# Strassen's algorithm in the last two token tiles of an attention and feed-forward kernel

## The chip, the core and the metric

The kernel runs on one core of one Trainium2 chip. The metric is the device time in microseconds of one launch; the time of the kernel before is the median of seven runs. The profile is that of one execution. Engines are written as in the profile: PE (TensorE, matrix multiplication; PEld is its weight load), DVE (VectorE), ACT (ScalarE), POOL (GpSimd), SP (SyncE, which issues the DMAs here).

## What is computed

```python
batch, n_heads, seq, head_dim = (8, 8, 576, 64)
# attention: heads 0-3 with a local mask of 32 positions, heads 4-7 with a strided one
scores = np.where(masks[None], scale * np.matmul(q, k.transpose(0, 1, 3, 2)), -1000000000.0)
attn = softmax(scores)
x = np.matmul(attn, v).transpose(0, 2, 1, 3).reshape(B * S, H * D)      # 4608 x 512
# feed-forward
a = x @ w1            # 512 x 1024
b = x @ w2            # 512 x 1024
h = a * b @ w3        # 1024 x 1024
out = h @ w_out       # 1024 x 512, float32
```

Inputs and output are float32. The kernel computes with fp16 operands and float32 sums, and multiplies w3 by w_out first, since nothing stands between them; the feed-forward part is then (a * b) @ w34.

## The kernel before

**Layout.** The attention output is kept transposed as `xT`, four tiles of 128 channels (one pair of heads each) by 4608 tokens. The weights are `w1h` and `w2h` (four chunks of 128 channels by 1024) and `w34` (eight blocks of 128 d_ff rows by 512). The feed-forward part goes over nine tiles of 512 tokens (loop at line 940). A tile has eight d_ff blocks `jc`. For each block, `ps_a` is summed over four matmuls of 128x512 (line 956), copied to SBUF by ACT (`asb`, line 964, traced at its helper's line 309), `ps_b` is summed over four more (line 972), and DVE multiplies the two into `abt` (line 978). Then four output pieces of eight matmuls each (line 992) are copied to `osb` by ACT and stored by SP (line 1013). A batch has 576 tokens, so tile 7 (tokens 3584 to 4095) reads batches 6 and 7 and tile 8 (4096 to 4607) reads batch 7 alone.

**Attention.** For each of eight batches (line 689) and four pairs of heads: scores on PE (line 794), exp on ACT (lines 808 and 811), mask on DVE (line 818), the product with v on PE (lines 830 and 840), and the normalisation. For the strided pairs that is a logarithm and an exp on ACT (lines 874 and 885) and two DVE multiplications into `xT` (line 901); for the local ones DVE (lines 863 and 864), a transpose on PE (line 921) and a copy. q, k and v arrive as float32 in staging tiles `stgs` (eight of 128x1024 float32), and POOL casts nearly all of them to fp16 (traced at line 313).

**Order.** Nothing in the order is left to chance: `Plan` (line 54) holds every piece of work as an `Op` with an estimated duration for each engine that may take it, its dependencies, the buffers that it takes and gives back, and a rank. `Plan.order` (line 89) walks through time with these estimates; whenever an engine is free it takes, among the operations that are ready and have their buffers, the one of lowest rank (lines 176 to 188). The sequence that comes out is emitted and each engine keeps to it. Matmuls marked `soft` have to have been ready for 100 ns by the estimates (`slack`, line 182). Operations marked `lock` on DVE and POOL are laid one after the other (line 212).

**Ranks.** Tile t has rank 100 + 24 t + 2 jc + 1 for the a matmuls of block jc (line 959), just above it for b, and 100 + 24 t + 17 + 2 ts for output piece ts (line 998). Attention of batch b has ranks from `_arank` (line 19), which lay the four head pairs over the span of the tile that is computed meanwhile.

**PSUM.** Eight banks: four single ones (kind "f", used by a, b and output matmuls among others) and two pairs (kind "B", scores and attention products). An "f" bank of `ps_a` comes free with the copy, one of `ps_b` with the multiplication.

## Time and profile before

| what | value |
|---|---|
| median of seven runs | 273.12 us |
| lowest and highest | 271.87 and 275.29 us |
| the profiled execution | 271.87 us |
| its span | 270.2 us |
| granted clock of PE over the span | 1.0 |
| PE, busy and share of the span | 258.9 us, 96% |
| DVE | 169.7 us, 63% |
| ACT | 156.0 us, 58% |
| POOL | 146.3 us, 54% |
| chain that ended last: share on PE | 83% |
| a, b and output matmuls' shares in that chain | 22%, 22%, 21% |

How to read it: the span is what the profiler saw of the program, and the time of the same execution is 1.7 us longer. An engine's busy time is the sum of its instructions; where it is under 100%, the rest is waiting or having nothing to do. A row of the profile names a line, an engine, an operation, what it writes and reads, shapes, and a count; then the busy time in us, the mean duration of one in ns, and the engine's idle time just ahead of them with what ended it. Matmuls overlap: a row's mean (379 ns for a 128x512 one) is longer than the distance between two starts, and the distance is what PE can do. Times in the instruction lists are start and length in us.

### The profile page before, as it was taken

Reading aid. Unit: us, or ns where it says so; the run is one execution under the profiler, and the core shown is the slowest. Engines: PE = TensorE matmul, PEld = TensorE weight load, DVE = VectorE, ACT = ScalarE, POOL = GpSimd, SP = SyncE. Lnnn points to the kernel's source line nnn. Section 1 sums busy time; section 2 is a strip of 40 time slices with the busy share of each in tenths; the row PEclk is TensorE's granted clock in tenths of the full one; section 3 lists DMA queues with packets and bytes.
Section 4 is the critical chain, followed back from the end, with each engine's and each line's share of the span. In section 5 each row is a group of like instructions: output and inputs, shape, how many; then the busy total and the mean of one; then the engine's idle time right before and its main releaser. Section 6 shows DMA issues by size and latency. Waiting matters only on the chain.

```text
span 270.2 us, 6083 instructions
## 1 busy us (share of the span) xinstructions
PE 258.9 (96%) x2265; PEld 141.3 (52%) x2265; DVE 169.7 (63%) x324; ACT 156.0 (58%) x280; POOL 146.3 (54%) x172
## 2 busy tenths in 40 slices
PE   7787899999999999999999999999999999999994
PEld 2466787545565555544544554455455554444443
DVE  6745566885787758766884788487669762422321
ACT  2770467764676764775577647756764774333331
POOL 6676996689979447955794289626980000000000
PEclk9999999999999999999999999999999999999999
DMA  7999999999799899899999998999996013003004
GB/s 244 336 359 284 307 361 353 317 252 292 266 271 227 135 273 217 197 182 290 194 196 197 273 169 198 173 276 199 194 208 139 0 41 116 2 21 136 0 4 155
DMA packets 72766, 54.41 MB, mean 201 GB/s; under 512 B 44256, under 2 KB 62048, under 8 KB 72736
## 3 DMA queue, kind: packets, MB, share of 16 engines
q1 hardware_dynamic: 72736, 54.02, 82.1%
q8 instruction: 18, 0.29, 0.5%
q14 instruction: 12, 0.10, 0.2%
HBM read 38.93 MB, written 9.44 MB: 179 GB/s over the span
## 4 chain that ended last, share of the span: by engine, by line
PE 83%; DMA 9%; issue 2%; ACT 2%; POOL 1%; SPq 1%; DVE 1%; POOLq 0%; ACTq 0%
PE ps_b L972 22%; PE ps_a L956 22%; PE ps_o L992 21%; DMA st<-in_moe_w_dram 5%; PE ps_S L794 4%; PE ps_mm L669 3%; PE ps_X L840 3%; PE ps_X L830 2%; PE ps_U L921 2%; DMA st<-in_k_dram 2%; DMA out_dram<-osb 2%; PE ps_T L747 1%; SPq L316 1%; POOL w3n L313 1%; PE ps_tr L649 1%
## 5 line engine op out<-in xcount | busy, mean ns | idle before, releaser
L972 PE MATMUL ps_b<-xT,w2h 128*128 128x512 f16 x288 | 73.8, 379 | 0.2 <-DVE kTL L311 0.2
L956 PE MATMUL ps_a<-xT,w1h 128*128 128x512 f16 x288 | 73.9, 379 | 0.0
L978 DVE TENSOR_TENSOR abt<-ps_b,asb 128x512 f16<-128x512 f32 x72 | 49.7, 690 | 38.4 <-PE ps_b L972 35.5
L309 ACT COPY asb<-ps_a 128x512 f32<-128x512 f32 x72 | 42.1, 586 | 49.5 <-PE ps_a L956 49.2
L992 PE MATMUL ps_o<-w,abt 128*128 128x512 f16 (+2 forms) x304 | 67.3, 368 | 0.0
L313 POOL CAST xs<-st 80x1024 f16<-80x1024 f32 (+1 forms) x36 | 33.4, 941 | 19.5 <-DMA st<-in_q_dram 16.7
L972 PEld LDWEIGHTS <-w2h 128*128 128x128 f16 x288 | 26.7, 98 | 28.6 <-issue 0.7
L992 PEld LDWEIGHTS <-abt 128*128 128x128 f16 x304 | 27.2, 98 | 27.6
L956 PEld LDWEIGHTS <-w1h 128*128 128x128 f16 x288 | 26.5, 98 | 27.5
L811 ACT ACTIVATE ps_S<-ps_S 128x576 f32<-128x576 f32 (+2 forms) x56 | 32.9, 627 | 12.2 <-PE ps_S L794 11.6
L309 ACT COPY osb<-ps_o 128x512 f32<-128x512 f32 (+1 forms) x36 | 20.8, 577 | 23.8 <-PE ps_o L992 21.0
L901 DVE TENSOR_TENSOR xT<-ps_X,rcp 64x288 f16<-64x288 f32 x56 | 25.2, 450 | 13.6 <-ACT rcp L885 12.8
L313 POOL CAST v16L<-st 32x768 f16<-32x768 f32 (+1 forms) x32 | 26.3, 821 | 6.6 <-DMA st<-in_v_dram 3.8
L818 DVE TENSOR_TENSOR ptm<-ps_S,maskL 128x576 f16<-128x576 f32 x28 | 19.9, 751 | 9.4 <-ACT ps_S L811 9.3
L864 DVE TENSOR_TENSOR xqs<-ps_X,rcq 96x384 f16<-96x384 f32 (+1 forms) x36 | 20.5, 568 | 1.2
L313 POOL CAST v16S<-st 72x1024 f16<-72x1024 f32 (+1 forms) x16 | 16.4, 1035 | 6.0 <-DMA st<-in_v_dram 6.0
L885 ACT ACTIVATE rcp<-ps_X 64x576 f32<-64x576 f32 x28 | 18.1, 647 | 0.9
L874 ACT ACTIVATE ps_X<-ps_X 64x576 f32<-64x576 f32 x28 | 17.7, 632 | 0.3
L669 PE MATMUL ps_mm<-woh,xT 128*128 128x256 f16 x128 | 16.0, 273 | 1.5 <-POOL woh L313 1.5
L840 PEld LDWEIGHTS <-ptm 128*96 128x96 f16 (+1 forms) x224 | 14.5, 124 | 5.5 <-issue 0.2
L313 POOL CAST x<-st 128x1024 f16<-128x1024 f32 x14 | 14.4, 1037 | 3.8 <-DMA st<-in_q_dram 1.9
L311 DVE COPY xT<-ps_U 128x576 f16<-128x576 f16 x18 | 8.8, 490 | 11.3 <-PE ps_U L921 11.3
(82 smaller groups left out, 265.9 us busy)
## 6 DMA issues: line engine op xcount, KB each, us to landing
out_dram<-osb SPq DMA_DIRECT2D x35, 256.0 KB
st<-in_moe_w_dram SPq DMA_DIRECT2D x16, 512.0 KB
st<-in_v_dram SPq DMA_DIRECT2D x16, 288.0 KB
st<-in_v_dram SPq DMA_DIRECT2D x16, 256.0 KB
st<-in_q_dram SPq DMA_DIRECT2D x7, 512.0 KB
st<-in_k_dram SPq DMA_DIRECT2D x7, 512.0 KB
st<-in_q_dram SPq DMA_DIRECT2D x10, 256.0 KB
st<-in_k_dram SPq DMA_DIRECT2D x10, 256.0 KB
```

The source lines that it names most:

```text
L309: pin(nc.scalar.copy(out=out, in_=in_))
L313: pin(nc.gpsimd.tensor_copy(out=out, in_=in_))
L669: pin(nc.tensor.matmul(ps, w3T(kc)[:, js], big["woh"][:, kc, ns], start=(kc == 0), stop=(kc == KF - 1)))
L811: pin(nc.scalar.activation(out=sps, in_=sps, func=AF.Exp, bias=0.0, scale=scale))
L818: pin(nc.vector.tensor_mul(ptm[0:kr, 0:576].rearrange("p (h a x) -> p h a x", h=2, x=w), pte[0:kr].rearrange("p h (a x) -> p h a x", x=w), ...
L840: pin(nc.tensor.matmul(xps[0:w, h, i * 65:(i + 1) * 65], ptms[pslot][0:kr, c0:c0 + w], vt[0:kr, 2 * (hp % 2) + h, g * m + i, 0:D + 1], sta ...
L864: pin(nc.vector.tensor_mul(xqs[0:w, 0:m].rearrange("p i h d -> p h i d"), xv[:, :, :, 0:D], _ap(rcp, 0, [[rcp.ap[0][0], w], [4, 2], [1, m] ...
L901: pin(nc.vector.tensor_mul(o, i0, i1))
L956: pin(nc.tensor.matmul(ps, w1h[:, ci, js], xT[ci][:, tok], start=(ci == 0), stop=(ci == KM - 1)))
L972: pin(nc.tensor.matmul(ps, w2h[:, ci, js], xT[ci][:, tok], start=(ci == 0), stop=(ci == KM - 1)))
L978: pin(nc.vector.tensor_mul(big[("abt", t)][:, jc, :], bank("f", f"b{t}_{jc}"), live[("asb", t, jc)]))
L992: pin(nc.tensor.matmul(ps, big[("abt", t)][:, ci, bass.ds(ts * P, P)], w34[:, ci, bass.ds(n0, nw)], start=(ci == 0), stop=(ci == KF - 1)))
```

## The change

Tiles 7 and 8 (`tA` and `tB`) are computed together. With X11, X12 the two channel halves of tile 7, X21, X22 those of tile 8, and W the matrix with w1 and w2 side by side, split in its channel halves, the four blocks a(7), b(7), a(8), b(8) are a 2x2 product of 2x2 blocks. For seven of the eight d_ff blocks (1 to 7; `sf`) it is formed in the way of Strassen and Winograd, with seven products of two matmuls in place of eight. Block 0 of both tiles stays as it was.

- **Sums of weights** T1 to T4 (fp16, 128x2x1024, kept in staging tiles), each in two halves of 512 columns, all on POOL. The first halves (columns for blocks 1 to 3) depend on the last load, the second halves (blocks 4 to 7) on a `gate`, a small POOL copy that depends on the last sum of inputs.
- **Sums of inputs** S1 to S4 (fp16, 128x2x512 each, in two pieces c): both pieces of S3 and the first pieces of S1, S2 and S4 on POOL, the second pieces of S1, S2 and S4 on DVE. They need `xT` of batch 7 and 6.
- **Products** P1 to P7: P1, P6, P7 and P4 are added up in one "f" bank (A); P5 and then P3 in one half of a "B" pair (G); P2 in the other (E). Between them: ACT copies A after P1 (`e`; in blocks 1 and 2 to SBUF, later straight into E), after P6 (`u2`), G after P5 (`p5`) and, from block 3 on, E after P2 (`c11`). DVE adds `u2` to G in place (`u4`), `p5` to A into SBUF (`c22`), in blocks 1 and 2 also the copy to E (`c11`), and multiplies: `h1` = G times c11 into tile 7's `abt`, `h2` = A times c22 into tile 8's. P6 waits for e, P7 for u2, P3 for u4, P4 for c22. The "B" pair is held from P5 to h1, the "f" bank from P1 to h2.
- **Ranks.** Block n (0 to 6) of the Strassen stage starts at 268 + 3n; block 0 of tile 7 has 269, that of tile 8 has 293; the output matmuls of both tiles are put 16 further back and also depend on every P5. The attention of batches 2 to 7 is moved back by 2.
- The new branch `xb` for the attention products' bank keeps to "B" with this configuration.

```diff
-    base = {0: 40, 1: 60}.get(b, 100 + 24 * (b - 1) - 4)
+    base = {0: 40, 1: 60}.get(b, 100 + 24 * (b - 1) - 2)
...
-           first=('DVE', 'ACT', 'POOL'), early=0, pm=4, nx=4, nstg=8, new=(2, 3), lb=3, ll=4, nat={'POOL': 1160})
+           first=('DVE', 'ACT', 'POOL'), early=0, pm=4, nx=4, nstg=8, new=(2, 3), lb=3, ll=4, nat={'POOL': 1160}, sf=(1, 2, 3, 4, 5, 6, 7), te={'POOL': 2150}, nr=(1, 25, 2, 0), te1='POOL', se=((3, 0), (3, 1), (1, 0), (2, 0), (4, 0)))
...
-    plan = Plan(dict(f=NF, B=2, stg=NSTG, asb=2, osb=3, rcp=2, xqs=2, xqd=cfg.get("nxq", 2), w3n=3, abt=NABT))
+    plan = Plan(dict(f=NF, B=2, stg=NSTG, asb=2, osb=3, rcp=2, xqs=2, xqd=cfg.get("nxq", 2), w3n=3, abt=NABT,
+                     u2=2, p5=2, c11=2, c22=2))
...
+    SF = cfg.get("sf", ())
+    tA, tB = NTILE - 2, NTILE - 1
+    tk1, tk2 = bass.ds(tA * NT, NT), bass.ds(tB * NT, NT)
+    smul, sfirst = {}, []
+    if SF:
+        W = {(1, 1): w1h[:, 0:2], (1, 2): w2h[:, 0:2], (2, 1): w1h[:, 2:4], (2, 2): w2h[:, 2:4]}
+        T, Tt = {}, {}
+        scr = consts.tile([P, 2], FP16, name="scr")
+        lastload = plan.loads[-1]
+        allw = [c for jc in range(KF) for c in w1c[jc] + w2c[jc]]
+        hw = DF // 2
+        for i, x, y in ((1, (1, 2), (1, 1)), (3, (2, 2), (1, 2)), (2, (2, 2), 1), (4, (2, 1), 2)):
+            for hf in range(2):
+                cs = bass.ds(hf * hw, hw)
+                def ftt(e, i=i, x=x, y=y, cs=cs, hf=hf):
+                    if hf == 0:
+                        Tt[i] = stgs[plan.slot[("stg", f"T{i}")]].bitcast(FP16).rearrange("p (k n) -> p k n", k=2)
+                    b0 = Tt[y] if isinstance(y, int) else W[y]
+                    eng = nc.gpsimd if e == "POOL" else nc.vector
+                    pin(eng.tensor_sub(Tt[i][:, :, cs], W[x][:, :, cs], b0[:, :, cs]))
+                T[(i, hf)] = plan.op(f"T{i}_{hf}", cfg.get("te", {"POOL": 2400}) if hf == 0 else {"POOL": 2150} if cfg.get("te1", "POOL") == "POOL" else {"DVE": 690}, ftt,
+                                     deps=allw + [lastload] + ([T[(y, hf)]] if isinstance(y, int) else [])
+                                     + ([T[(i, 0)]] if hf else []),
+                                     take=[] if hf else [("stg", f"T{i}")], rank=11 + hf, lock=True)
+        Sx, St = {}, {}
+        xd = lambda h, bs: [x for b in bs for x in xTop[(b, h)]]
+        b1, b2 = range(tA * NT // S, (tB * NT - 1) // S + 1), range(tB * NT // S, B)
+        for i in (3, 1, 2, 4):
+            for c in range(2):
+                def fss(e, i=i, c=c):
+                    eng = nc.gpsimd if e == "POOL" else nc.vector
+                    if (i // 3) not in St:
+                        St[i // 3] = stgs[plan.slot[("stg", f"S{i // 3}")]].bitcast(FP16).rearrange(
+                            "p (i k n) -> p i k n", i=2, k=2)
+                    sv = lambda j: St[j // 3][:, (j - 1) % 2 if j < 3 else j - 3, c]
+                    if i == 3:
+                        a0, a1, op = xT[c][:, tk1], xT[c][:, tk2], eng.tensor_sub
+                    elif i == 1:
+                        a0, a1, op = xT[c][:, tk2], xT[2 + c][:, tk2], eng.tensor_add
+                    elif i == 2:
+                        a0, a1, op = sv(1), xT[c][:, tk1], eng.tensor_sub
+                    else:
+                        a0, a1, op = xT[2 + c][:, tk1], sv(2), eng.tensor_sub
+                    pin(op(sv(i), a0, a1))
+                d = {3: xd(c, b1) + xd(c, b2), 1: xd(c, b2) + xd(2 + c, b2), 2: xd(c, b1), 4: xd(2 + c, b1)}[i]
+                if i in (2, 4):
+                    d = d + [Sx[(i // 2, c)]]
+                Sx[(i, c)] = plan.op(f"S{i}_{c}", {"POOL": 1150} if (i, c) in cfg.get("se", ()) else {"DVE": 430}, fss, deps=d + [lastload] + ([Sx[(i, 0)]] if c else []),
+                                     take=[("stg", f"S{i // 3}")] if c == 0 and i in (1, 3) else [], rank=0.5, lock=True)
+                if c == 0 and i in (2, 4):
+                    Sx[(i, c)].deps.append(Sx[(i - 1, c)])
+        if cfg.get("te1", "POOL") == "POOL":
+            gate = plan.op("gate", {"POOL": 200}, lambda e: pin(
+                nc.gpsimd.tensor_copy(out=scr, in_=St[1][:, 1, 1, 0:2])), deps=[Sx[(4, 1)], T[(4, 0)]], rank=11)
+            for i in range(1, 5):
+                T[(i, 1)].deps.append(gate)
+        SL = lambda j: (lambda c: St[j // 3][:, (j - 1) % 2 if j < 3 else j - 3, c])
+        A = {1: lambda c: xT[c][:, tk1], 2: lambda c: xT[2 + c][:, tk1], 4: lambda c: xT[2 + c][:, tk2]}
+        sd = lambda i: [Sx[(i, 0)], Sx[(i, 1)]]
+        TAG = dict(u2="q0", p5="k0", c11="q1", c22="k1")
+        seen = {}
+    zs = {}
+    for t in (tA, tB) if SF else ():
+        def fz(e, t=t):
+            big[("abt", t)] = ffn.tile([P, KF, NT], FP16, tag="abt", bufs=NABT, name="abt")
+        zs[t] = plan.op(f"abt{t}", {"PE": 0}, fz, deps=xd(0, b1), take=[("abt", f"abt{t}")], rank=100 + 24 * t - 20)
+    for n_, jc in enumerate(SF):
+        js = bass.ds(jc * P, P)
+        hf = jc * P // hw
+        prods = dict(P1=(A[1], lambda: W[(1, 1)], "A", xd(0, b1) + xd(1, b1)),
+                     P5=(SL(1), lambda: Tt[1], "G", sd(1) + [T[(1, hf)]]),
+                     P6=(SL(2), lambda: Tt[2], "A", sd(2) + [T[(2, hf)]]),
+                     P2=(A[2], lambda: W[(2, 1)], "E", xd(2, b1) + xd(3, b1)),
+                     P7=(SL(3), lambda: Tt[3], "A", sd(3) + [T[(3, hf)]]),
+                     P4=(A[4], lambda: Tt[4], "A", xd(2, b2) + xd(3, b2) + [T[(4, hf)]]),
+                     P3=(SL(4), lambda: W[(2, 2)], "G", sd(4)))
+        kA, kB = ("f", f"Aw{jc}"), ("B", f"Bw{jc}")
+        def bk(x, kA=kA, kB=kB):
+            return bank(*kA) if x == "A" else bank(*kB)[:, "EG".index(x)]
+        R = 100 + 24 * tA + 3 * n_
+        tmp = {}
+        def new(nm, tmp=tmp):
+            tmp[nm] = qkp.tile([P, NT], FP32, tag=TAG[nm], bufs=2, name=nm)
+            return tmp[nm]
+        def prod(nm, extra=(), take=(), rank=0, kA=kA, kB=kB, js=js, prods=prods, bk=bk, n_=n_):
+            lf, rt, x, d = prods[nm]
+            def fn(e):
+                if nm == "P1":
+                    bank(*kA, [P, NT], FP32)
+                if nm == "P5":
+                    if plan.slot[kB] in seen:
+                        live[kB] = seen[plan.slot[kB]]
+                    else:
+                        assert n_ < 2
+                        seen[plan.slot[kB]] = bank(*kB, [P, 2, NT], FP32)
+                st_ = nm in ("P1", "P5") or nm == "P2" and n_ < 2
+                for c in range(2):
+                    pin(nc.tensor.matmul(bk(x), rt()[:, c, js], lf(c), start=st_ and c == 0,
+                                         stop=c == 1, skip_group_check=not st_))
+            return plan.op(f"{nm}w{jc}", {"PE": 432}, fn,
+                           deps=[x_ for x_ in d + list(extra) if x_], take=take, rank=rank, soft=True)
+        def vec(nm, eng, fn, deps, give=(), take=()):
+            return plan.op(f"{nm}w{jc}", {eng: 590 if eng == "ACT" else 690}, fn, deps=deps, give=list(give),
+                           take=[(x, f"{x}w{jc}") for x in take], rank=3 + .1 * n_)
+        tk = {x: (x, f"{x}w{jc}") for x in TAG}
+        q1 = prod("P1", take=[kA], rank=R, extra=list(zs.values()))
+        q5 = prod("P5", take=[kB], rank=R + .1, extra=[q1])
+        sfirst.append(q5)
+        if n_ < 2:
+            ce_ = vec("e", "ACT", lambda e, bk=bk, new=new: copy("ACT", new("c11"), bk("A")), [q1], take=["c11"])
+        else:
+            ce_ = vec("e", "ACT", lambda e, bk=bk: copy("ACT", bk("E"), bk("A")), [q1, q5])
+        q6 = prod("P6", extra=[ce_], rank=R + .5)
+        c5 = vec("p5", "ACT", lambda e, bk=bk, new=new: copy("ACT", new("p5"), bk("G")), [q5], take=["p5"])
+        q2 = prod("P2", extra=[q5 if n_ < 2 else ce_], rank=R + .6)
+        cu = vec("u2", "ACT", lambda e, bk=bk, new=new: copy("ACT", new("u2"), bk("A")), [q6], take=["u2"])
+        q7 = prod("P7", extra=[cu], rank=R + 1)
+        g = vec("u4", "DVE", lambda e, bk=bk, tmp=tmp: pin(nc.vector.tensor_add(bk("G"), bk("G"), tmp["u2"])),
+                [cu, c5], give=[tk["u2"]])
+        if n_ < 2:
+            c11 = vec("c11", "DVE", lambda e, bk=bk, tmp=tmp: pin(
+                nc.vector.tensor_add(tmp["c11"], bk("E"), tmp["c11"])), [q2, ce_])
+        else:
+            c11 = vec("c11", "ACT", lambda e, bk=bk, new=new: copy("ACT", new("c11"), bk("E")), [q2], take=["c11"])
+        c22 = vec("c22", "DVE", lambda e, bk=bk, new=new, tmp=tmp: pin(
+            nc.vector.tensor_add(new("c22"), bk("A"), tmp["p5"])), [q7, c5], take=["c22"], give=[tk["p5"]])
+        q3 = prod("P3", extra=[g], rank=R + 1.1)
+        q4 = prod("P4", extra=[c22], rank=R + 1.2)
+        h1 = vec("h1", "DVE", lambda e, bk=bk, tmp=tmp, jc=jc: pin(
+            nc.vector.tensor_mul(big[("abt", tA)][:, jc, :], bk("G"), tmp["c11"])), [q3, c11],
+                 give=[kB, tk["c11"]])
+        h2 = vec("h2", "DVE", lambda e, bk=bk, tmp=tmp, jc=jc: pin(
+            nc.vector.tensor_mul(big[("abt", tB)][:, jc, :], bk("A"), tmp["c22"])), [q4], give=[kA, tk["c22"]])
+        smul[(tA, jc)], smul[(tB, jc)] = h1, h2
+    def frk(t, jc):
+        if not SF or t < tA:
+            return 100 + 24 * t + 2 * jc + 1
+        i = [x for x in range(KF) if x not in SF].index(jc)
+        return 100 + 24 * tA + cfg.get("nr", (1, 25, 2, 0))[t - tA] + cfg.get("nr", (1, 25, 2, 0))[2] * i
...
+            a = plan.op(f"a{t}_{jc}", {"PE": 864}, fa, deps=[z] + w1c[jc] + (xd if t in zs else []), take=[("f", f"a{t}_{jc}")],
+                        rank=frk(t, jc))
...
+                                deps=[muls[4 * hf + i] for i in range(4)] + w34op[8 * hf:8 * hf + 8] + [h] + (sfirst if t >= tA else []),
+                                take=[("f", key)] if hf == 0 else [], rank=100 + 24 * t + 17 + 2 * ts + 0.001 * hf + (16 if SF and t >= tA else 0),
```

## The prediction

> **What bounds the kernel now.** I read the page's engine totals first, then its 40 slices, then the table by stretches, and last the instructions in order of time around the start of the last two tiles. The engine totals:
>
> ```profile
> PE 258.9 (96%) x2265; PEld 141.3 (52%) x2265; DVE 169.7 (63%) x324; ACT 156.0 (58%) x280; POOL 146.3 (54%) x172
> ```
>
> The slices (6.76 us each), PE, POOL and clock rows:
>
> ```profile
> PE   7787899999999999999999999999999999999994
> ...
> POOL 6676996689979447955794289626980000000000
> PEclk9999999999999999999999999999999999999999
> ```
>
> PE is full from slice 6 to the end at full clock. GpSimd does nothing in the last ten slices. The stretches (length, then busy us and instruction count of PE, PEld, DVE, ACT, POOL; the last two are tiles 7 and 8, the one ahead of them is tile 6 with the last batch's attention):
>
> ```profile
> 202.60:224.73 22.13, 22.13 (x189) 11.18 (x187) 15.88 (x30) 14.17 (x24) 0.00 (x0) 1.00 0.27 68
> 224.73:245.45 20.72, 20.72 (x98) 9.37 (x97) 5.53 (x8) 7.02 (x12) 0.00 (x0) 1.00 0.14 52
> 245.45:266.40 20.95, 20.92 (x113) 10.28 (x111) 5.92 (x9) 7.24 (x13) 0.00 (x0) 1.00 0.15 56
> ```
>
> Tiles 7 and 8 are 41.7 us in which PE never waits, while DVE is busy 11.5 us and ACT 14.3. So PE's instruction count sets the end, and DVE and ACT have about 27 us each to give. Removing a matmul there is worth its whole slot, as long as what replaces it keeps PE fed.
>
> **What it removes.** In order of time a group of four 128x512 matmuls starts every 0.865 us (225.59 after 224.73), so a slot is 0.216 us. For each of 7 d_ff blocks the two tiles together need 2 x 8 = 16 matmuls now, and 7 products of 2 = 14 afterwards. 7 x 2 x 0.216 = **3.02 us**, 1.1% of the kernel. The output matmuls (64 x 0.216 = 13.8 us) and block 0 stay. More than 3.02 us is not to be had.
>
> **What it adds on DVE and ACT.** Rows of one operation each:
>
> ```profile
> L978 DVE TENSOR_TENSOR abt<-ps_b,asb 128x512 f16<-128x512 f32 x72 | 49.7, 690 | 38.4 <-PE ps_b L972 35.5
> L309 ACT COPY asb<-ps_a 128x512 f32<-128x512 f32 x72 | 42.1, 586 | 49.5 <-PE ps_a L956 49.2
> ```
>
> Per block, where there were two copies and two multiplications: blocks 1 and 2 need 3 copies (e, p5, u2) and 5 DVE operations (u4, c11, c22, h1, h2); blocks 3 to 7 need 4 copies and 4 DVE operations. Every one reads 512 PSUM columns, as the rows do; that some also write PSUM is not in the trace for DVE, but on ACT it is (L811 writes 576 columns to PSUM in 636 ns, L808 to SBUF in 648), so I give it no price. DVE: 2 x 5 + 5 x 4 + 2 (block 0) = 32 x 0.69 = 22.1 us. ACT: 6 + 20 + 2 = 28 x 0.586 = 16.4 us. PE in the same stage: 7 x 14 x 0.216 + 16 x 0.216 (block 0 of both tiles) = 21.2 + 3.5 = **24.6 us**. So DVE goes from 27% to 90% of this stage. PE remains the longest, narrowly.
>
> Here a rule speaks against the change: the Trainium skill (VectorE: DVE Perf Modes, The DRAIN you can't avoid) says that a Vector operation does not start until the one ahead has left the pipe. Then DVE needs its 22.1 us plus hand-overs. The trace has the case:
>
> ```profile
> 206.68 0.69 DVE L978 TENSOR_TENSOR abt<-ps_b,asb 128x512 f16<-128x512 f32 x1
> 207.29 0.18 DVE L863 RECIPROCAL rcq<-ps_X 96x6 f32<-96x6 f32 x1
> ```
>
> The second starts 0.61 us after the first, not 0.69. By the rule DVE's load is 22.1 us, by the row 32 x 0.61 = 19.5; I take the row for operations that are ready, and keep 22.1 for the range. Both are below 24.6.
>
> **The hand-overs.** Within a block the products depend on each other through ACT and DVE. The prices of a hand-over:
>
> ```profile
> 225.59 1.03 PE L972 MATMUL ps_b<-xT,w2h 128*128 128x512 f16 x4
> 225.79 0.58 ACT L309 COPY asb<-ps_a 128x512 f32<-128x512 f32 x1 [0.28 <-PE ps_a L956]
> ...
> 226.72 0.69 DVE L978 TENSOR_TENSOR abt<-ps_b,asb 128x512 f16<-128x512 f32 x1 [3.43 <-PE ps_b L972]
> ```
>
> The a group gave up PE at 225.59 and ACT began at 225.79: 0.20 us. The b group gave it up at 226.45 (0.865 later) and DVE began at 226.72: 0.27. ACT's end to PE's start:
>
> ```profile
> 13.37 0.45 ACT L309 CAST kTS<-ps_R 128x128 f16<-128x128 f32 x1 [0.38 <-DVE kTS L311]
> ...
> 13.88 0.43 PE L794 MATMUL ps_S<-qT,kTS 64*128 64x72 f16 x16 [0.19 <-ACT kTS L309]
> ```
>
> 13.82 to 13.88: 0.06 us. The scarce thing is the pair of two-bank B slots: one is held from P5 to h1, so two blocks are in flight and a block may hold it 2 x 3.03 = 6.05 us. Its chain from P5's start: P5 0.43 + 0.20 + copy e 0.59 + 0.06, P6 0.43 + 0.20, copy u2 0.59 + 0.06, u4 0.69 + 0.06, P3 0.43 + 0.27, h1 0.69 + 0.06 = 4.76 us. That leaves 1.3 us for waiting in the queues of three engines. I laid one block into 7 PE slots of 0.433 us by hand, repeating every 3.03: P1, P5 in slots 0 and 1, P6 and P2 in 4 and 5, P7 in 9, P3 in 10, P4 in 13. These are all different modulo 7, every hand-over above is met, and the four DVE operations fall without overlap. A gapless order exists. It is tight (P6 has no room and the slot is free 0.4 us before it is wanted), and the planner takes what is ready, so I allow waits. Two covers absorb some: block 0 of tile 8 (1.73 us) has a later rank than the Strassen blocks and may run whenever PE would wait, and the last block's chain lies under output matmuls of tile 7, which may start after the last P5. Without the cover by block 0, waits would count in full. I put waits at 2 us before cover (0.3 per block), 0.4 after it: an estimate, from 0 (the gapless order) to 2.
>
> **GpSimd.** Eight sums of weights (2 inputs, 128x1024) and five of inputs (128x512); the trace has no two-input operation on GpSimd. Nearest row:
>
> ```profile
> L313 POOL CAST w3n<-st 128x1024 f16<-128x1024 f32 x8 | 8.2, 1037 | 3.6 <-DMA st<-in_moe_w_dram 3.6
> ```
>
> One input costs 1.04 us, so at least 1.04, and with two passes over its input 2.1. The Trainium skill (GPSIMD Engine Reference, Elementwise — side-by-side cycle accounting) speaks against placing them there: about 2.6 cycles an element for two inputs, 1024 x 2.6 / 1.2 GHz = 2.2 us each as an estimate. I take 2.2; the row shows how much room there is. The first four (8.9 us) fit between GpSimd's last cast at 202.6 and 211.5, when nobody waits. The second four start after the gate at about 225 and end at 234; block 4, their first reader, begins near 224.7 + 1.7 + 3 x 3.0 = 235.4 and reads the last one in its last product. They would have to cost over 3 us each to be late. Cost: nothing, hidden by blocks 1 to 3. Were that cover gone, the first would cost its own 2.2 us. Slowing DVE? The stretches for L978 alone, with GpSimd 74% busy (18.51 of 25 us) and idle, show 8 in 5.52 and 5.53 us:
>
> ```profile
> 150.00:175.00 25.00, 5.52 (x8) 1.00 1.05 207
> ...
> 245.45:266.40 20.95, 5.53 (x8) 1.00 0.15 56
> ```
>
> **The start of the stage.** Block 1's P5 needs the input sums, and these need the last head pair:
>
> ```profile
> 222.38 0.91 DVE L901 TENSOR_TENSOR xT<-ps_X,rcp 64x288 f16<-64x288 f32 x2 [0.31 <-ACT rcp L885]
> ```
>
> It ends at 223.29; GpSimd's halves of S1 and S2 read earlier pairs (ready at 216.25) and are done by then. DVE's half of S1 is put at 0.43 us by the change's own cost; the 0.69 of the f32 row is its upper bound. P5 is ready at 223.29 + 0.04 + 0.43 + 0.06 = 223.8. PE has tile 6's outputs until 224.73, then P1 of three blocks (1.3 us). Attention ranks move back by 2, at most one a and b pair (1.73 us): P5 at 225.6, cover to 226.0. Cost 0; if the cover were gone, up to 1.7 us. No DMA is added, moved or passed; SP's queue keeps its order. Eight stores now come in one row of 13.8 us instead of two rows of four; they keep the spacing of 1.73 us, so 0.
>
> **The sum** against the profiled execution: 270.2 - 3.02 + 0.4 = 267.6 us of span, with 1.7 us outside it (271.87 - 270.2) 269.3. That execution is the fastest of the seven; the median is 1.25 us above it, so against 273.12 I forecast **270.5 us**.
>
> **Rivals.**
> (B) The waits eat half: 0.5 us a block, 3.5, less 1.73 of cover: gain 1.2, 271.9. For it: 90% on DVE and a loop with 1.3 us of room. Against it: 0.61 us spacing.
> (C) It doesn't do what it says: fewer matmuls, but all the saved slots come back as PE waiting, 273.1. That needs 4.75 us of waiting, 0.68 a block.
> (D) Slower: the loop through the two B slots becomes the bound. It decides from a pair cycle above 6.05 us; if every one of its seven hand-overs costs 0.35 us more than the rows say, because ACT and DVE are found busy, the cycle grows by about 2.2 us to 7.3, 0.6 a block at first, and with the copy c11 and c22 queued ahead of u4 and h1 by another 0.6. At 1.2 a block: 8.4 - 1.73 - 3.02 = 3.7 slower, 276.8. Against it: the rows of ACT and DVE are exact to 2%.
>
> **How the numbers follow.** The main case 0.60, B 0.20, C 0.08, D 0.12. The main case spreads from 269.7 (no waits beyond the covered, 3.0) to 271.1, and the seven runs of before lie 3.4 us apart, which moves a median by some 0.5. A measurement of this kernel tells about 1% (2.7 us) from no change, and the full saving is just above that, so two thirds of the main case count as faster: 0.60 x 0.7 = 0.42. Slower is D, 0.12; the rest, 0.46, is within 1%. The range: below 269.2 only a gain beyond 3.02 with a lucky median; above, it takes in B and C up to 273.6 and leaves out D.
>
> **What would show it.** Right: PE's count 14 lower, the two tiles' stretch about 39 us with PE at 98% or more, DVE near 90% in its first 25 us, GpSimd rows near 2.2 us that nobody waits for. Wrong: PE waits on u2, u4 or c22 adding to over 2 us (B, C), DVE with the next operation always ready (D), or two-input rows on GpSimd above 3 us.

## The result, and the profile after

| | before | after |
|---|---|---|
| median of all runs | 272.60 us (63 runs, 271.06 to 275.29) | 270.53 us (26 runs, 269.64 to 271.81) |
| ratio to before, 95% interval | | 0.9926, 0.9913 to 0.9940 |
| profiled execution, its span | 271.87, 270.2 us | 270.64, 268.5 us |
| PE instructions | 2265 | 2251 |

The change makes the kernel 0.74% faster, 2.0 us (1.6 to 2.4): less than the 2.6 us of the forecast's sum. That the forecast time of 270.5 was met is luck: the seven runs that it started from had a median of 273.12, 0.5 us above that of all 63, and from 272.60 the same sum gives 270.0.

The engine totals of the kernel after, and three rows of its slices (6.71 us each):

```profile
PE 256.9 (96%) x2251; PEld 140.3 (52%) x2251; DVE 178.9 (67%) x342; ACT 162.1 (60%) x293; POOL 169.0 (63%) x186
...
PE   7878799999999999999999999999999999999994
...
POOL 6586897679969716955796379627999553900000
PEclk9999999999999999999999999999999999999999
```

PE has 14 instructions fewer, GpSimd now works until slice 35, and the clock is full throughout. The table by stretches (length, then busy us and instructions of PE, PEld, DVE, ACT, POOL), cut where the stage begins (224.88), at 245.45 as in the table of before, and where the last output matmuls run out:

```profile
202.60:224.88 22.28, 22.28 (x193) 11.42 (x192) 16.87 (x33) 14.16 (x24) 12.34 (x9) 1.00 0.19 56
...
224.88:245.45 20.57, 20.21 (x92) 8.87 (x91) 14.24 (x24) 12.84 (x23) 8.56 (x5) 1.00 0.10 38
245.45:264.70 19.25, 19.15 (x105) 9.39 (x103) 7.26 (x13) 7.59 (x14) 0.00 (x0) 1.00 0.24 89
```

The two tiles take 39.8 us instead of 41.7, and PE, which never waited there before, is idle in both rows. These idle times are small, and a matmul's modelled end hides part of each, so I took them from the starts: one product of two matmuls takes 0.43 us, and whatever lies between two starts beyond that is a wait. Over the two tiles that is 0.01 us before and **1.12 us after**. The account closes: 3.02 (14 slots) - 1.12 = 1.90, less 0.15 because the stage begins at 224.88 and not at 224.73, makes 1.75; the spans differ by 1.7.

Where PE waits. Matmuls of block 3, in order of time (start, length):

```profile
234.09 0.59 PE L1053 MATMUL ps_Bw<-st,st 128*128 128x512 f16 x2
234.52 0.59 PE L1053 MATMUL ps_Aw<-xT,w1h 128*128 128x512 f16 x2
235.35 0.59 PE L1053 MATMUL ps_Aw<-st,st 128*128 128x512 f16 x2 [0.23 <-ACT ps_Bw L310]
235.96 0.59 PE L1053 MATMUL ps_Bw<-xT,w1h 128*128 128x512 f16 x2
...
237.25 0.59 PE L1053 MATMUL ps_Aw<-st,st 128*128 128x512 f16 x2
237.96 0.59 PE L1053 MATMUL ps_Bw<-st,w2h 128*128 128x512 f16 x2
```

These are P5, the P1 of a later block, P6 (0.83 after that P1, so 0.39 waited), P2 (0.61 after P6, 0.19 waited), P7, and P3 (0.71 after P7, 0.28 waited). The other waits are 0.15 us ahead of block 1's P2 and twice 0.06. ACT and DVE beside it:

```profile
234.72 0.57 ACT L310 COPY ps_Bw<-ps_Aw 128x512 f32<-128x512 f32 x1 [2.38 <-PE ps_Bw L1053]
235.33 0.58 ACT L310 COPY p<-ps_Bw 128x512 f32<-128x512 f32 x1
235.97 0.58 ACT L310 COPY u<-ps_Aw 128x512 f32<-128x512 f32 x1
236.59 0.58 ACT L310 COPY c<-ps_Bw 128x512 f32<-128x512 f32 x1
```

```profile
237.21 0.70 DVE L1076 TENSOR_TENSOR ps_Bw<-ps_Bw,u 128x512 f32<-128x512 f32 x1 [1.03 <-ACT c L310]
```

P6 waits for copy e, which writes P1's result into E. P1 was done long before, but e itself waited until P5, which writes G, was out of PE (234.72). P2 writes E. It begins at 235.96, 0.05 us after copy p5 (235.91), which reads G. u4 adds u2 into G; u2 is there at 236.55, DVE is idle, and still u4 begins at 237.21, 0.04 us after copy c11 (237.17), which reads E. Neither needs the other's half. Of all seven u4, this is what the trace says that DVE's idle time before them ended with (us, times):

```profile
  ACT c L310: 2.9, 5
```

Five of five u4 in the blocks where ACT does c11 follow that copy. My theory: E and G are two halves of one PSUM tile of two banks, and waits are kept for the tile, not for its banks. So products and additions wait for work on the other half. The rivals: the queues of ACT and DVE are the delay (their order is poor), or the ordinary block of tile 8, which was to fill such gaps, is spent too early; half of it stands at 226.61, ahead of the first product (227.47):

```profile
226.61 1.03 PE L1119 MATMUL ps_a<-xT,w1h 128*128 128x512 f16 x4
227.47 1.03 PE L1053 MATMUL ps_Aw<-xT,w1h 128*128 128x512 f16 x4
...
244.06 1.03 PE L1135 MATMUL ps_b<-xT,w2h 128*128 128x512 f16 x4
```

### The profile page after: what moved, and what is told of

It reads as the page before. It is cut to its first block, busy times and chain, and to the rows that moved or that the text cites. A ratio compares the mean times of both kernels' runs of the same rounds, so it can differ in the third digit from the quotient of the medians.

```text
span 268.5 us, 6079 instructions
## 1 busy us (share of the span) xinstructions
PE 256.9 (96%) x2251; PEld 140.3 (52%) x2251; DVE 178.9 (67%) x342; ACT 162.1 (60%) x293; POOL 169.0 (63%) x186
## 4 chain that ended last, share of the span: by engine, by line
PE 84%; DMA 9%; POOL 1%; ACT 1%; DVE 1%; SPq 1%; issue 1%; POOLq 0%; ACTq 0%
PE ps_o L1155 22%; PE ps_b L1135 19%; PE ps_a L1119 18%; DMA st<-in_moe_w_dram 6%; PE ps_Aw L1053 4%; PE ps_S L795 4%; PE ps_Bw L1053 3%; PE ps_mm L670 3%; PE ps_X L843 3%; PE ps_X L831 3%; PE ps_U L924 2%; DMA st<-in_q_dram 2%; PE ps_T L748 2%; DMA out_dram<-osb 1%; SPq L317 1%
## 5 line engine op out<-in xcount | busy, mean ns | idle before, releaser
L1135 PE MATMUL ps_b<-xT,w2h 128*128 128x512 f16 x232 | 59.4, 379 | 0.2 <-DVE kTL L312 0.2
L1119 PE MATMUL ps_a<-xT,w1h 128*128 128x512 f16 x232 | 59.6, 379 | 0.0
L310 ACT COPY asb<-ps_a 128x512 f32<-128x512 f32 x58 | 34.0, 588 | 31.0 <-PE ps_a L1119 30.0
L1141 DVE TENSOR_TENSOR abt<-ps_b,asb 128x512 f16<-128x512 f32 x58 | 39.9, 688 | 7.6 <-PE ps_b L1135 6.4
L1135 PEld LDWEIGHTS <-w2h 128*128 128x128 f16 x232 | 21.6, 98 | 23.6 <-issue 0.7
L1119 PEld LDWEIGHTS <-w1h 128*128 128x128 f16 x232 | 20.2, 99 | 18.5
L819 DVE TENSOR_TENSOR ptm<-ps_S,maskK 72x576 f16<-72x576 f32 x20 | 14.1, 746 | 2.6 <-ACT ps_S L812 2.6
```

Source lines behind the costliest of these rows:

```text
L310: pin(nc.scalar.copy(out=out, in_=in_))
L819: pin(nc.vector.tensor_mul(ptm[0:kr, 0:576].rearrange("p (h a x) -> p h a x", h=2, x=w), pte[0:kr].rearrange("p h (a x) -> p h a x", x=w), ...
L1119: pin(nc.tensor.matmul(ps, w1h[:, ci, js], xT[ci][:, tok], start=(ci == 0), stop=(ci == KM - 1)))
L1135: pin(nc.tensor.matmul(ps, w2h[:, ci, js], xT[ci][:, tok], start=(ci == 0), stop=(ci == KM - 1)))
L1141: pin(nc.vector.tensor_mul(big[("abt", t)][:, jc, :], bank("f", f"b{t}_{jc}"), live[("asb", t, jc)]))
```

## The experiments

In the table, waits are those of PE in the last two tiles, read as above; ratio is against the kernel before.

| kernel | median, us | ratio, 95% interval | span | waits, us |
|---|---|---|---|---|
| after | 270.53 | 0.9926 (0.9913 to 0.9940) | 268.5 | 1.12 |
| no hand-overs | 269.56 | 0.9910 (0.9886 to 0.9934) | 267.7 | 0 |
| first products early | 270.60 | 0.9942 (0.9921 to 0.9963) | 267.8 | 1.43 |
| c11 after u4 | 270.32 | 0.9934 (0.9913 to 0.9954) | 268.4 | 1.53 |
| both | 271.22 | 0.9968 (0.9948 to 0.9989) | 269.4 | 2.05 |
| pair split | 269.65 | 0.9903 (0.9873 to 0.9934) | 267.6 | 0.01 |
| split, early products | 268.86 | 0.9896 (0.9850 to 0.9943) | 266.8 | 0 |
| the same again | 269.34 | 0.9891 (0.9850 to 0.9933) | 267.6 | 0.01 |
| split, early, all eight blocks | 268.59 | 0.9867 (0.9829 to 0.9906) | 266.4 | 0.26 |
| all eight blocks | 271.26 | 0.9958 (0.9932 to 0.9984) | 271.1 (its longest run) | 2.38 |
| early gate | 271.04 | 0.9940 (0.9910 to 0.9969) | 269.4 | 1.22 |
| late sums on VectorE | 279.65 | 1.0252 (1.0201 to 1.0303) | 277.4 | 3.55 |

**Is it the hand-overs at all?** The four copies and the sums u4, c11 and c22 are left out, and the two multiplications read an input tile in place of c11 and c22; the seven products follow one another directly. The output is then not the right one; the run is for the time alone.

```diff
-        q6 = prod("P6", extra=[ce_], rank=R + .5)
+        q6 = prod("P6", extra=[q1], rank=R + .5)
...
-        q3 = prod("P3", extra=[g], rank=R + 1.1)
-        q4 = prod("P4", extra=[c22], rank=R + 1.2)
+        q3 = prod("P3", extra=[q5], rank=R + 1.1)
+        q4 = prod("P4", extra=[q7], rank=R + 1.2)
```

> The changed kernel with its products alone: the copies e, p5, u2, c11 and the sums u4 and c22 are left out, so nothing stands between the products of a block, and the two multiplications read an input tile in place of c11 and c22. The output is not the reference's. PE issues the same 114 matmuls in the a/b/product stage. Theory (the saving of 14 matmul slots is whole, and the changed kernel gives 1.1 us of it back in PE waits inside the Strassen stage): PE waits in the stage under 0.2 us, 3.0 us less than before, ratio to before 0.989. Rival (the saving itself is smaller: the matmuls onto half-filled banks or the later attention cost something): no faster than the changed kernel, 0.9926.

PE has no wait left. So the 14 matmuls are worth their whole slots, and what is missing in the kernel after is lost in what stands between the products. Whether that is the hand-overs or the load that the copies and sums put on ACT and DVE, this run does not tell.

**Order or cover?** Two edits of the order, alone and together: the empty operation that reserves tile 8's buffer gets an earlier rank, so that the first products may go ahead of tile 8's ordinary block; and c11's copy is queued behind u4.

```diff
-        zs[t] = plan.op(f"abt{t}", ..., rank=100 + 24 * t - 20)
+        zs[t] = plan.op(f"abt{t}", ..., rank=100 + 24 * tA - 20)
...
-            c11 = vec("c11", "ACT", ..., [q2], take=["c11"])
+            c11 = vec("c11", "ACT", ..., [q2, g], take=["c11"])
```

> The changed kernel with one rank altered: the zero-length operation that reserves tile 8's product buffer gets tile 7's rank, so the first product of block 1 may go ahead of block 0. In the changed kernel a and b of block 0 of tile 7 and a of tile 8 (2.6 us of PE work) ran first, while DVE and ACT had little to do, and were gone when PE waited 0.7 us around blocks 2 and 3. Theory (waits come from the order: cover spent early): PE waits in the stage fall from 1.1 to about 0.6 us, ratio to before 0.9908. Rival (DVE's load is the bound, whatever the order): still 0.9926. Rival (block 0 first was needed to cover the input sums): waits at the start instead, 0.993 or more.

> The changed kernel with one dependency added: from block 3 on the copy c11 (bank E) is ordered after the sum u4 (bank G of the same pair). In the changed kernel every u4 of these blocks started when the copy c11 of the other half had ended, though it does not read it. Theory (waits between the two halves of a pair lengthen the chain that holds the pair by about 0.6 us): u4 starts at the end of u2 instead, P3 and the release of the pair come earlier, PE waits in the stage fall by 0.3 us, ratio 0.9915. Rival (the copy c11, now late, makes h1 wait instead): no gain or a loss, 0.9926 to 0.994.

> Both edits of the two runs before: the reserving operation early, and c11 after u4. Theory: the two causes are different (order of the filler, and the wait across a pair's halves), so the effects add: PE waits in the stage 0.3 us or less, ratio 0.9900, close to the kernel without hand-overs. Rival (one cause, DVE): as the changed kernel, 0.9926.

Three misses: the waits grew to 1.43, 1.53 and 2.05 us. With early products, PE's two longest waits are P2's behind p5, in blocks 1 and 2 (0.46 and 0.41 us):

```profile
226.53 0.59 PE L1053 MATMUL ps_Bw<-xT,w1h 128*128 128x512 f16 x2 [0.30 <-ACT p L310]
...
231.25 0.59 PE L1053 MATMUL ps_Bw<-xT,w1h 128*128 128x512 f16 x2 [0.24 <-ACT p L310]
```

The ordinary block, set free, did not go there: its a matmuls moved to 242.58, its b matmuls to 245.60. The planner lays a filler where its own estimates show a gap, and they know nothing of a wait for the other half. Reordering moves such waits and does not remove them. So two changes of the order did not help, which speaks against both rivals without excluding a better order.

**The pair split.** E and G become PSUM tiles of one bank each, in a pool that is opened when attention is done. The order of work stays: in the two traces every engine has the same instructions in the same order (2251 on PE, 293 on ACT, 342 on DVE, 186 on GpSimd).

```diff
-            return bank(*kA) if x == "A" else bank(*kB)[:, "EG".index(x)]
+            return bank(*kA) if x == "A" else bank(*kB)["EG".index(x)]
...
-                        seen[plan.slot[kB]] = bank(*kB, [P, 2, NT], FP32)
+                        if not seen:
+                            psb.close()
+                            psx[0] = psb.enter_context(tc.tile_pool(name="pss", bufs=1, space=bass.MemoryType.PSUM, reuse_waits="tile"))
+                        i = plan.slot[kB]
+                        live[kB] = seen[i] = [psx[0].tile([P, NT], FP32, tag=f"{x}{i}", name=f"ps_{x}w{i}") for x in "EG"]
```

> The changed kernel in its own order, with one edit: when attention is done, the two-bank pairs become four tiles of one bank each, so that E and G of a block are separate tiles. Semaphores then order only instructions that touch the same bank: P2 no longer waits for the copy p5 (it did in blocks 1 and 3: 0.15 and 0.19 us of PE), u4 no longer for the copy c11 (0.28 us in block 3). Theory (false waits across a pair's halves and a gap that the order itself has are two causes): in the stage these three waits go, the one of 0.39 us ahead of block 3's P6 stays; PE waits 0.5 us instead of 1.1, ratio to before about 0.9905. Rival (the chain is bound by DVE or ACT being busy): the waits move elsewhere, ratio 0.9926 as the changed kernel.

The waits are gone to the last, also the 0.39 us ahead of block 3's P6 that was expected to stay: copy e writes E, and no longer waits for P5, which writes G. In the kernel after it began at 234.72; here it begins 2 us ahead of P5 (234.03), as soon as P1 is done:

```profile
232.07 0.57 ACT L313 COPY ps_Ew<-ps_Aw 128x512 f32<-128x512 f32 x1 [0.59 <-PE ps_Aw L1060]
```

The stage's first 24.6 us, after:

```profile
224.70:249.30 24.60, 24.24 (x111) 10.67 (x110) 17.45 (x30) 14.99 (x27) 8.56 (x5) 1.00 0.09 33
```

and with the pair split:

```profile
224.80:249.40 24.60, 24.60 (x116) 11.17 (x115) 18.50 (x31) 15.35 (x29) 8.56 (x5) 1.00 0.09 33
```

PE does 116 matmuls in the time of 111: five slots, 1.08 us. Two rows show what changed (line numbers are 7 higher for u4 and 3 for copies), ACT's c11 and DVE's u4 of block 3:

```profile
236.06 0.59 ACT L313 COPY c<-ps_Ew 128x512 f32<-128x512 f32 x1
```

```profile
236.20 0.70 DVE L1083 TENSOR_TENSOR ps_Gw<-ps_Gw,u 128x512 f32<-128x512 f32 x1 [0.18 <-ACT u L313]
```

u4 starts 0.03 us after u2's end (236.17), while c11's copy runs on until 236.65. With the order unchanged and all waits gone, this settles the cause: the order was good enough, and what PE lost it lost to waits for the other half of the tile.

**The filler.** With all eight blocks in Strassen's form there are two matmuls fewer again (0.43 us), and no ordinary block to fill gaps. Run on the kernel after, and on the split kernel with early products, which was also run by itself, twice:

```diff
-... sf=(1, 2, 3, 4, 5, 6, 7), ...
+... sf=(0, 1, 2, 3, 4, 5, 6, 7), ...
```

> The changed kernel with Strassen's products in all eight blocks of d_ff: two matmuls fewer (0.43 us), and no block 0 in the old form to put where PE would wait. Theory (block 0 works as filler, though an imperfect one): PE waits rise from 1.1 to about 1.7 us, more than the 0.43 saved, ratio 0.993 to 0.994. Rival (the filler does nothing, since it ran too early): waits stay at 1.1, ratio 0.991.

> The split pair, and the reserving operation of tile 8 early, so that the first products go ahead of block 0. With the pair undivided this order gave 1.4 us of PE waits, of which 0.87 us were P2 waiting for p5 in blocks 1 and 2 and 0.55 us P3 waiting for u4 in blocks 4 and 5. Theory: the order was good and lost to false waits; with the pair split the 0.87 go wholly, PE waits are 0.3 to 0.5 us, ratio 0.990. Rival (this order leaves no room, whatever the tiles): waits stay above 1 us, 0.993.

> All three edits together: bank pair split into tiles of one bank each, the first products ahead of tile 8's first matmul, and all eight blocks in Strassen's form, so two matmul slots fewer (2 x 0.216 = 0.43 us) and no ordinary filler block. Theory (the waits were false waits between the halves of a pair, so with single-bank tiles no filler is needed): waits of the last two tiles under 0.4 us, ratio 0.988 against the kernel before, 0.4 us under the split kernel with early products. Rival (the filler's 1.7 us of matmuls also cover true waits at the start of the chain): waits rise by more than 0.43 us, ratio 0.990 or more.

> The split kernel with early products once more, for a narrower interval beside the version with all eight blocks: 268.9 us, ratio 0.9896, waits of the last two tiles 0.

With the joint pair, the waits go from 1.12 to 2.38 us, more than the 0.43 saved; the ratio is 0.9958, a little worse than expected. With the pair split they are 0.26, less than the 0.43 saved. This is the fastest kernel of the study, at 0.9867 (0.9829 to 0.9906), 1.3% under the kernel before; its interval overlaps those of the two runs with seven blocks. The early products give nothing that the waits show (0 with and without them); the 0.8 us between the spans of two runs of one and the same kernel (266.8 and 267.6) is as large as their difference to the split alone. 0.66 of it lies ahead of the stage, which begins at 224.44 in one and at 225.10 in the other. So differences of some tenths between spans say little here, and the waits inside the stage say more.

**GpSimd's place.** The second halves of the weight sums are put on VectorE, and no gate is needed (`te1='DVE'`).

> The changed kernel with the second halves of the four sums of weights on DVE instead of GpSimd (four fp16 operations of 128x1024, no gate); everything else by the planner. Theory (GpSimd's time was free, DVE's is not): they fall into the attention of the last batch, where DVE stands in the chain to the last channels; four of about 0.6 to 0.7 us delay the last xT by 2.7 us, and PE has no work to put there. Ratio to before 1.003, the gain gone. Rival (GpSimd's placement is beside the point, DVE has 27 us idle in the two tiles): as the changed kernel, 0.9926.

A clear miss: 7 us slower than the kernel before. VectorE's first and second such sum:

```profile
205.36 7.09 DVE L965 TENSOR_TENSOR st<-w2h,w1h 128x1024 f16<-128x1024 f16 x1
...
217.98 0.68 DVE L965 TENSOR_TENSOR st<-w2h 128x1024 f16<-128x1024 f16 x1
```

GpSimd's row meanwhile:

```profile
204.53 2.12 POOL L965 TENSOR_TENSOR st<-w2h 128x1024 f16<-128x1024 f16 x1
206.61 2.12 POOL L965 TENSOR_TENSOR st<-w2h,st 128x1024 f16<-128x1024 f16 x1
208.69 1.15 POOL L990 TENSOR_TENSOR st<-xT 128x512 f16<-128x512 f16 x1
209.79 2.11 POOL L965 TENSOR_TENSOR st<-w1h,st 128x1024 f16<-128x1024 f16 x1
```

A sum of 0.68 us lasts 7.09, until 0.55 us after the last of GpSimd's ends (211.90). Behind it in DVE's queue is an attention mask, and PE waits for that:

```profile
213.18 0.54 PE L843 MATMUL ps_X<-v16L,ptm 128*96 128x65 f16 x6 [4.97 <-DVE ptm L819]
```

With 2.4 us more of waits in the last two tiles (two of them, 1.1 and 1.3 us, are P5's for the last attention result and for VectorE's input sum), and a granted clock of 0.93 in the stretch around it (20.0 us of PE busy time, so by estimate some 1.4 us), this gives 8.8 us of the 8.9 by which the span is longer than after's. The stretch:

```profile
200.00:225.00 25.00, 20.02 (x151) 10.03 (x150) 20.91 (x27) 11.02 (x20) 13.66 (x9) 0.93 0.32 67
```

The Trainium skill (SBUF — State Buffer, Who interferes with whom) says that a Vector instruction with both inputs in SBUF contends with a GpSimd instruction that reads SBUF. The trace agrees, and here VectorE did not get in at three ends of GpSimd instructions (206.65, 208.73 and 209.84).

**Is that what the gate keeps apart?** In the kernel after, the gate waits for VectorE's last input sum, so no weight sum of GpSimd lies over VectorE's three. Let it wait for GpSimd's own half:

```diff
-                nc.gpsimd.tensor_copy(out=scr, in_=St[1][:, 1, 1, 0:2])), deps=[Sx[(4, 1)], T[(4, 0)]], rank=11)
+                nc.gpsimd.tensor_copy(out=scr, in_=St[1][:, 1, 0, 0:2])), deps=[Sx[(4, 0)], T[(4, 0)]], rank=11)
```

> The gate ahead of GpSimd's late sums waits for the first half of S4 (GpSimd's own) instead of its second half (VectorE's), so the four two-input T sums run on GpSimd from about 221.4 to 230 us and lie over VectorE's own three weight sums (0.42 us each from 224.4). Theory (a VectorE sum with two inputs in SBUF does not run while GpSimd runs two-input sums back to back): one of VectorE's 0.42 us sums lasts until about 230, P5 of block 1 starts near 230.4 rather than 228.3, about 2 us are lost, ratio 1.000. Rival (the two engines take turns by instruction): one GpSimd sum of 2.1 us at most stands ahead of it, which tile 8's ordinary block covers, ratio 0.993 as in the changed kernel.

VectorE's three input sums, and GpSimd's row under them:

```profile
225.21 1.67 DVE L990 TENSOR_TENSOR st<-xT,xT 128x512 f16<-128x512 f16 x1
226.92 2.23 DVE L990 TENSOR_TENSOR st<-st,xT 128x512 f16<-128x512 f16 x1
...
229.67 1.74 DVE L990 TENSOR_TENSOR st<-xT,st 128x512 f16<-128x512 f16 x1
```

```profile
224.48 2.12 POOL L965 TENSOR_TENSOR st<-w2h 128x1024 f16<-128x1024 f16 x1
226.56 2.31 POOL L965 TENSOR_TENSOR st<-w2h,st 128x1024 f16<-128x1024 f16 x1
228.94 2.19 POOL L965 TENSOR_TENSOR st<-w1h,st 128x1024 f16<-128x1024 f16 x1
```

The rival was right. The sums take 1.7 to 2.2 us instead of 0.42, but each waits for one GpSimd sum, ends 0.28 us after it, and so gets in; the GpSimd sums that follow are 0.19 and 0.07 us longer than 2.12. PE's waits are 1.22 us (1.12 in the kernel after), since the sums end before the products ask for them. Without the gate's order the change would have lost little: of the 0.9 us by which this span is longer than after's, 0.8 lies ahead of the stage, which begins at 225.68.

**Why there through a row, and here one apiece?** VectorE's late sums again, in two halves of 128x512 each, the size that got in.

```diff
-                    pin(eng.tensor_sub(Tt[i][:, :, cs], W[x][:, :, cs], b0[:, :, cs]))
+                    for k in ((slice(0, 1), slice(1, 2)) if e == "DVE" else (slice(0, 2),)):
+                        pin(eng.tensor_sub(Tt[i][:, k, cs], W[x][:, k, cs], b0[:, k, cs]))
```

> As the kernel with the late weight sums on VectorE, but each of these sums is two operations of 128x512 instead of one of 128x1024. There the first of them took 7.09 us while GpSimd ran four sums with two inputs one after the other; in the kernel with the early gate VectorE's sums of 128x512 took 1.7 to 2.2 us each under such a row, one GpSimd sum apiece. Theory (the length of VectorE's operation decides whether it gets in between two GpSimd sums): the two halves last about 2.1 us each at most, 4.2 together, TensorE's wait of 4.97 us shrinks by about 3, ratio about 1.015. Rival (another thing decides, such as which engine asked first): the first half again lasts until GpSimd's row ends, ratio 1.025 as there.

The group of these two halves (shortest, median, longest ns):

```profile
L966 DVE TENSOR_TENSOR st<-w2h,w1h x2: 413/3027/5641, 206.1 to 211.7; 128x512 f16<-128x512 f16 x2
```

The first half lasted 5.64 us, again to the end of GpSimd's row (211.47, where it ends 0.29 us later), and the second 0.41. So the length does not decide it, and what does stays open. PE's wait behind it is 3.24 us, and the clock in the same stretch is 1.00:

```profile
200.00:225.00 25.00, 21.76 (x177) 10.74 (x176) 21.79 (x35) 12.50 (x22) 13.30 (x9) 1.00 0.24 65
```

In time this run is inconclusive: nine executions spread from 272.33 to 280.23 us and one took 669.90. The ratio of the four fastest, 1.007 (1.0011 to 1.0129), says little; the trace is of an execution of 277.45 us.

## Where the prediction held, and where not

- **What bounds, and what is removed: held.** PE sets the end, and its count fell by 14. Without hand-overs, or with the pair split, nothing of the 3.02 us is lost.
- **The load on DVE and ACT: held.** DVE's operations of the stage, in a row of three:

```profile
232.47 0.69 DVE L1076 TENSOR_TENSOR ps_Bw<-ps_Bw,u 128x512 f32<-128x512 f32 x1
233.06 0.68 DVE L1088 TENSOR_TENSOR abt<-ps_Bw,c 128x512 f16<-128x512 f32 x1
233.66 0.68 DVE L1091 TENSOR_TENSOR abt<-ps_Aw,c 128x512 f16<-128x512 f32 x1
```

  They start 0.59 and 0.60 us apart, so the row of 0.61 was the right one to choose, and not the rule as the prediction quotes it. The same section (VectorE: DVE Perf Modes, The DRAIN you can't avoid) goes on that a next operation that is not held starts earlier, which these rows show. In 24.6 us DVE is busy 17.45, or 71%, not near 90% as the last paragraph of the prediction had it; some of its operations also come later, the last h1 until 253.03. Writing to PSUM costs next to nothing (u4: 698 ns, the others 681 to 692).
- **The prices of a hand-over: held.** P6 gives up PE at 235.78 and ACT starts at 235.97 (0.19; predicted 0.20); p5 ends at 235.91 and P2 starts at 235.96 (0.05; predicted 0.06).
- **The waits after cover, 0.4 us: mis-sized; they were 1.12.** The step that failed is the list of what waits for what. "Its chain from P5's start" has one wait that the mathematics does not ask for, copy e behind P5, takes it as given, and has P6 without room behind it: that became the largest wait, 0.39 us. It lacks two others: in the kernel P2 waits for p5 as well, and u4 for c11. With the same prices: e ends 1.22 us after P5's start, p5 0.61 later at 1.83, P2 runs from 1.88 to 2.31, c11 follows u2 on ACT from 2.52 to 3.10, u4 from 3.14 to 3.84, P3 to 4.32, h1 from 4.59, and the pair is free at 5.34 instead of 4.76. That leaves 0.7 us of slack, not 1.3. Block 3 confirms it: P3 ends 4.30 us after P5 began. The split, which takes just these three kinds of wait away, ends all of PE's. That the measured time came close to the forecast is no proof of the list.
- **The cover by tile 8's ordinary block: failed.** Half of it ran at 226.61 ahead of all products, because the empty operation that P1 depends on had a late rank (272), and the other half at 244.06. It covers only what the planner foresees. In the split kernel without it (all eight blocks) the waits are 0.26 us, so the cover is worth little there.
- **GpSimd: held.** The forecast was 2.2 us for each sum, hidden. Four late ones in the kernel after:

```profile
225.95 2.13 POOL L965 TENSOR_TENSOR st<-w2h,w1h 128x1024 f16<-128x1024 f16 x1
228.04 2.12 POOL L965 TENSOR_TENSOR st<-w2h 128x1024 f16<-128x1024 f16 x1
230.12 2.12 POOL L965 TENSOR_TENSOR st<-w2h,st 128x1024 f16<-128x1024 f16 x1
232.32 2.13 POOL L965 TENSOR_TENSOR st<-w1h,st 128x1024 f16<-128x1024 f16 x1
```

  They end at 234.45, and no PE wait follows on one. "Slowing DVE?" was answered from a line that reads PSUM (L978), and for such lines the answer stands: DVE's u4, c22 and h1 lie over these sums at 0.68 to 0.70 us. For sums with both inputs in SBUF it is wrong. Here the gate keeps these apart; where it did not, PE's waits grew by 0.1 us (early gate), and with the late sums on VectorE the kernel lost 7 us.
- **The start of the stage: held.** VectorE's last input sum ends at 225.74 and the first P5 begins at 228.34, without a wait. (The first of these sums ended at 224.83, later than the 223.8 at which the prediction had P5 ready, and it cost nothing.)
- **The rivals.** B had the right kind of loss, too large: 1.12 us is 0.16 a block, not 0.25 after cover. C and D did not come: from P5's start to h1's end a block holds the pair for 5.4 to 7.4 us, 6.2 in the mean. That is about the 6.05 that the loop allows, but no wait of PE stands ahead of a P5, so the pair was not what it waited for. In D's own sum, seven times 0.35 us is 2.45 and the cycle 7.2, not 2.2 and 7.3; D stays where it was.

## What to carry to other kernels

Write the chain of waits from the tiles as they are allocated, not from the formula: two accumulators that share one tile wait for each other, and giving each its own tile won back here all that was lost (1.1 us) without touching the order. A filler in a planned order covers only gaps that the plan can see. Where two elementwise engines both read two SBUF operands, look in the trace for an operation many times its usual length before moving work between them.

## What the runs showed of the hardware

- A VectorE sum with both inputs in SBUF (0.68 us alone) lasted 7.09 us while GpSimd's row of two-input sums ran (four of its instructions), and one of 0.42 lasted 5.64; elsewhere such sums waited for one GpSimd sum each (1.67 to 2.23 us). What decides which was not found.
- GpSimd's two-input fp16 sum takes 2.12 us for 128x1024 and 1.15 for 128x512; two that followed a waiting VectorE sum took 2.31 and 2.19.
- ACT copies 128x512 float32 from one PSUM bank to another in 0.58 us, no slower than to SBUF (0.59).
- Around PE's wait of 4.97 us the granted clock of a 25 us stretch was 0.93; with late sums in halves, where that wait was 3.24 us, it was 1.00.
